# Plain queries and values in parts, and a new order of the first loads, in a fused attention and feed-forward kernel

## The chip, the cores and the metric

The kernel runs on one core of a Trainium2 chip. The metric is the device time of one execution in microseconds (us), the median of several runs. A core has five engines that run side by side: TensorE (PE: matmuls; PEld is its weight load), VectorE (DVE), ScalarE (ACT), GpSimd (POOL) and SyncE (SP), which here only issues DMA loads and stores. Each engine works off its own list in the order in which the program gives it and waits at semaphores for the others.

## The reference: what is computed

Eight batches with eight heads of 576 tokens and 64 columns go through windowed attention, and the result, 4608 rows of 512, through a feed-forward layer.

```python
mask_plain = (rel >= 0) & (rel < window)                                  # window 32, heads 0 to 3
mask_dil = (rel >= 0) & (rel < window * dilation) & (rel % dilation == 0)  # dilation 4, heads 4 to 7
...
scores = np.where(masks[None, :, :, :], scores, -1000000000.0)
attn = np.exp(scores - max);  attn = attn / sum(attn);  attn_out = attn @ v
...
h = x @ w_in                 # 512 -> 2048
g = np.maximum(0.01 * h, h)
return (g @ w_out)           # 2048 -> 512
```

Inputs and outputs are float32; the kernel computes in float16 operands with float32 sums.

## The kernel before

**Tiling.** Two batches share one activation buffer `xt` of 1152 token columns, which is cut into three chunks of 384. For each chunk the feed-forward layer runs 16 "ups" (`up`, L778: one block j of 128 hidden columns, four matmuls over the 512 inputs, weights `w_in`, result in a bank `hps`, leaky ReLU by ScalarE into `gt`, L803) and 12 "downs" (`down`, L827: three row tiles, each in four parts of four hidden blocks, weights `w_out`, L841). Chunk 0 holds the first 384 tokens of batch 0, chunk 1 those of batch 1, chunk 2 the last 192 tokens of both.

**Attention.** Heads come in pairs; a batch has two dilated pairs (hp 2, 3), then two plain pairs (hp 0, 1). Per pair, q and k are loaded into `stg`, cast to float16 in `nat` (L249), turned by TensorE into the bank `tp` (L557) and copied from there into `slots` (L507, L509). A unit of a pair is a score matmul into `sps` (L685; for the first two batches the mask is added by another matmul, L666), an exponential by ScalarE into `ee` (L691), for later units a mask multiply (L705), the value matmuls into `ops` (L729, L739, L749), and 1/sum as exp(-ln) by ScalarE into `rc` (L761, L763); the product goes into `xt` (L767). For batches 0 and 1 the units of the first 384 tokens ("part 0") come first, and the last 192 tokens ("part 1") later, with q and k reloaded in small pieces by `load_rest` (L389).

**Loads.** Nearly all loads go through one queue, issued by SyncE in a fixed order. The string `FIRST` (L20) gives the order of the early ones: b and v are q, k and values of batch 0 (dilated first, then plain), c and y the same of batch 1, i one of eight pieces of `w_in` (512 KB), o one of eight pieces of `w_out`, 0 and 1 the last tokens of a batch. `con` is a table of constants; its last part holds the mask multipliers. w_in pieces 1 to 4 hold hidden columns 0 to 1023 (ups 0 to 7), pieces 5 to 8 the rest; a piece gives 128 of the 512 inputs, so an up needs four pieces. Two pieces of w_out serve one part of the downs.

**Who sets the order.** The whole program is a list of tasks with engines, rough costs, dependencies and priorities. A planner (`_Plan.run`, L84) plays it through once while the kernel is built and so fixes each engine's order; nothing is reordered later. `RANKS` (L21) gives the priorities of the attention tasks of batch 0 part 0, part 1, batch 1 part 0, part 1 (start, step per pair). Where the planner expects a gap on TensorE before the first downs, it puts in filler matmuls on `warm` (L934), which compute nothing that is used.

Of the kernel before, what the change touches and what calls it, by code (L numbers as in the profile page):

```python
# [16 lines left out]
WHEN = (-5.0, 15.0, 50.0, 77.0, 112.0, 138.0, 172.0, 200.0)  # L17
CON = -1484.5
AFTER = -1495.0
FIRST = "bvbviiii0iicooiicoyoooooy1"  # L20
RANKS = ((10.0, 1.0), (10.0, 3.0), (20.0, 2.0), (40.0, 0.5))  # L21


def _constants():
# [113 lines left out]
def kernel(  # L138
# [94 lines left out]
                return n * (ta + (tb - ta) * (size - a) / (b - a)) / 16e3  # L233
        return n * size / 25.6 / 16e3

    def load(queue, dst, src, n, size, deps, prio):
        eng = ENG[queue]
        return plan.dma(queue, 0.7 if size == 128 else 0.48, took(n, size), deps,
                        lambda e: eng.dma_start(dst, src), prio,  # L239
                        LATE if prio > -1500 + len(FIRST) else 0.8 if prio >= AFTER else 0.0)  # L240

# [64 lines left out]
    def load_group(b, g, prio, prio_v):  # L306
# [28 lines left out]
        if dil and early:  # L335
            lv = [load("SP", at(vs, 0, 128, 0, [256, 4], [1, 256]),
                       dram(v, base, [4 * D, 128], [HS, 4], [1, 256]), 512, 1024, v_old, prio_v)]
            v_late[b] = vs, v_old, v_users
        elif dil:
            lv = [load("SP", at(vs, 0, 128, i * 256, [512, 4], [1, 256]),  # L340
                       dram(v, base + i * 64 * D, [4 * D, 128], [HS, 4], [1, 256]),
                       512, 1024, v_old, prio_v) for i in range(2)]
        elif early:
            lv = []
            for j in range(2):
                n = 12 - (first and j == 0)
                lj = [load("SP", at(vs, 0, 128, (12 * j + 12 - n) * D, [D, n], [1, D]),
                           dram(v, base + (1152 * j + 96 * (12 - n) - 32) * D, [D, 128], [96 * D, n],
                                [1, D]), 128 * n, 256, v_old, prio_v + 0.3 * j)]
                if n < 12:  # L350
                    lj += [load("SP", at(vs, PAD, 128, 0, [1, D]), dram(v, 0, [D, 96], [1, D]),
                                96, 256, v_old, prio_v), t_vz]
                lv.append(lj)
        else:
            lv = [load("SP", at(vs, 0, 128, 0, [D, 24], [1, D]),
                       dram(v, base - 32 * D, [D, 128], [96 * D, 24], [1, D]),
                       3072, 256, v_old, prio_v)]

        for j in range(2):
            nn, n_old = ring("NAT", NNAT, n_users := [])  # L360
            na, c_qk = nat[nn], []
            for o in range(2):
                st, s_users = stage[o]
                if early:
                    dst = at(na, 0, 128, o * 512, [D, 2], [128, 4], [1, D])
                    src = at(st, 0, 128, j * 512, [256, 2], [D, 4], [1, D])
                    n = 512
                else:
                    dst, src, n = na[:, o * S:o * S + S], st[:, j * S:j * S + S], S
                c_qk.append(cast(dst, src, n, (loads[o][j:j + 1] if first else loads[o]) + n_old, prio,  # L370
                                 (("ACT",) if o else ("DVE",)) if first and dil and j == 0 else
                                 CENG if early else ("POOL",)))
                s_users.append(c_qk[-1])
            dn, d_old = ring("VD" if dil else "VP", NV, d_users := [])
            vt = (vd if dil else vp)[dn]
            n_v = 384 if not dil else 256 if early else 512
            h_a, h_s = (2 * j * n_v, n_v) if early else (j * n_v, 2 * n_v)
            n, w = n_v // D, 128 * (8 if dil else 6)
            c_v = [cast(at(vt, 0, 128, 0, [w, 2], [128, n], [1, D]),
                        at(vs, 0, 128, h_a, [h_s, 2], [D, n], [1, D]), 2 * n_v,  # L380
                        (lv[j] if early and not dil else lv) + d_old, prio_v)]
            v_users += c_v
            seen_ones[b, 2 * g + j] = [t_ones["d" if dil else "p", dn]]
            kept[b, 2 * g + j] = vt, d_users
            visits[b, 2 * g + j, 0] = (na, c_qk, n_users, vt,
                                       c_v + ([t_one] if (b, 0) in TILED else
                                              [t_ones["d" if dil else "p", dn]]), d_users)

    def load_rest(b, prio):  # L389
# [5 lines left out]
        for o, src in ((0, q), (1, k)):  # L395
# [3 lines left out]
        c = cast(at(rest, 0, 128, 0, [128, 8], [D, 2], [1, D]),  # L399
                 at(st, 0, 128, 0, [D, 8], [0, 2], [1, D]), 1024, lo + r_old, prio)  # L400
        s_users.append(c)
        vs, v_old, v_users = v_late[b]
        spread = bass.AP(tensor=vs.tensor, offset=vs.offset + 1024,
                         ap=[[4 * vs.ap[0][0], 16], [256, 4], [1, 256]])
        lv = load("SP", spread,
                  dram(v, (b * H + 4) * HS + 512 * D, [4 * D, 16], [HS, 4], [1, 256]),
                  64, 1024, v_old + [t_vr], prio)
        for vi in (2, 3, 0, 1):
            vt, d_users = kept[b, vi]
            c_v = []  # L410
            if vi >= 2:
                c_v = [cast(at(vt, 0, 64, 0, [1024, 2], [128, 4], [1, D]),
                            at(vs, 0, 64, 1024 + (vi - 2) * 512, [256, 2], [D, 4], [1, D]), 512,
                            [lv] + d_users, prio + 30)]
                v_users += c_v
            visits[b, vi, 1] = rest, [c], r_users, vt, c_v + seen_ones[b, vi], d_users
# [3 lines left out]
    def load_w(n, prio):  # L420
# [10 lines left out]
        else:  # L431
            x = 1024 * (n - 8)
            src = dram(moe_w_out, 128 * x, [2 * DM, 128], [1, 1024])
            dst = w_out
        t = load("SP", st, src, 128, 4096, old, prio)
        for i in range(2):
            c = cast(dst[:, x + 512 * i:x + 512 * i + 512], st[:, 512 * i:512 * i + 512], 512, [t],
                     prio, ("POOL",) if 4 <= n < 8 else CENG)
# [71 lines left out]
        cost = {"DVE": 0.1 + n * 0.00065, "ACT": 0.08 + n * 0.00095}  # L510
        return add(tuple((e, cost[e]) for e in eng), None, 0.2, deps, fn, prio)

    slot_of, turned_rest, pair_moves = {}, {}, {}
    held = {t.name: [] for t in banks["S0"] + banks["O0"]}

    def arranged(dil, u0, u1):
# [6 lines left out]
    def turn(b, hp, part, prio):  # L523
# [50 lines left out]
        def k_to(bank, i, p0, p1, lo, hi, deps, eng=("DVE",)):  # L574
            n = hi - lo
            if dil:
                o, od, id_ = lo, [[144, 4], [1, n]], [[128, 4], [1, n]]
            else:
                o, od, id_ = PAD + 4 * lo, [[4, n], [1, 4]], [[1, n], [128, 4]]
            return [move(at(kb, p0, p1, o, *od), at(bank, p0, p1, i, *id_), 4 * n,  # L580
                         deps + old + zk, prio, eng)]

        if part == 1:
            if hp == 2:
# [26 lines left out]
            q_users += new  # L611
            ev += new
        else:
            _, q_old = ring("TP", 1, q_users := [])
            tq = add("PE", 0.23, 0.25, c_qk[:1] + [t_id] + q_old, turn_in(tpb, na, 0), prio, 0.2)
            n_users.append(tq)
            for lo, hi in ((0, 128),) if dil else ((0, 120), (120, 128)):
                q_users += q_to((lo, lo), lo, hi, [tq])
            if b == 0:
                _, k_old = ring("TPK", 1, k_users := [])  # L620
                kb_in, c_in, k_eng = tpk, 0, ("DVE", "ACT")
            else:
                k_old, k_users, kb_in, c_in, k_eng = q_old, [], tpb[:, 512:1024], 512, ("DVE",)
            tk = add("PE", 0.23, 0.25, [c_qk[1], t_id] + k_old, turn_in(kb_in, na, 512), prio, 0.2)
            n_users.append(tk)
            k_users += k_to(tpk if b == 0 else tpb, c_in, 0, 128, 0, 128,
# [3 lines left out]
            else:  # L630
                for t in q_users:
                    t.deps.append(tk)
                q_users += k_users
            ev += q_users + k_users
        slot_of[b, hp] = tn, users, ev
        return ev, users, qb, kb

# [347 lines left out]
```

The softmax here doesn't subtract the row's maximum and nothing guards it: scores larger than these inputs give would overflow.

## Time and profile before

| what | value |
|---|---|
| time, median of 3 runs | 317.56 us (317.21 to 317.59) |
| span of the profiled execution | 314.2 us |
| TensorE busy | 303.7 us (97%) |
| ScalarE / VectorE / GpSimd busy | 219.7 / 174.2 / 120.4 us |
| DMA queue of SyncE | 50.46 MB in 157,696 packets, 67.3% of 16 engines' span |
| chain that ended last | PE 83%, DMA 7%, ACT 4%, SyncE's queue 3% |

The page cuts the span into 40 slices of 7.85 us and gives the busy share of each engine as a digit (9 is 90% or more). A group or timeline line reads: start and length in us (timeline), engine, source line, operation, output tile <- input tiles, shape, count, and in brackets the idle time of the engine before it and who ended it. The answers by stage give the stretch, its length, and then the busy time of PE, PEld, DVE, ACT and POOL with the number of instructions in brackets, the granted clock of TensorE, the share of DMA engines busy and the data rate. The chain of waits gives start, length and the work that held the end back at that time.

### The profile page before, as it was taken

The numbers are of one execution on the slowest core, as the hardware profiler recorded it, in microseconds if no ns is written. First come the engines' busy times: TensorE is split into PE (matmuls) and PEld (weight loads), VectorE is DVE, ScalarE is ACT, GpSimd is POOL, SyncE is SP. The second block draws the span as 40 slices with busy tenths as digits, with TensorE's granted clock in tenths as the row PEclk, the third lists the DMA queues.
The fourth block names the chain that finished last, engine by engine and source line by source line (L and its number), as shares of the span: only waits on it lengthen the run. The fifth ranks groups of instructions, "written<-read, shape, count | busy, mean of one in ns | idle before, by whom it ended". The sixth has DMA issues, their size and how long they took to land.

```text
span 314.2 us, 6332 instructions
## 1 busy us (share of the span) xinstructions
PE 303.7 (97%) x2257; PEld 179.6 (57%) x2257; DVE 174.2 (55%) x396; ACT 219.7 (70%) x501; POOL 120.4 (38%) x174
## 2 busy tenths in 40 slices
PE   7968999999999999999999999999999999999995
PEld 3625555667777656655555555555555555555544
DVE  5856894557896687857858667654433420000011
ACT  3925674889998999987888888787887743334310
POOL 4466655464584463935819447450000000000000
PEclk9999999999999999999999999999999999999999
DMA  7999999999999399999989978711111111211113
GB/s 247 326 331 407 401 318 190 259 193 207 239 217 189 119 222 180 229 174 206 192 185 197 179 208 147 169 35 33 35 33 35 33 35 46 53 37 35 33 33 100
DMA packets 158175, 51.14 MB, mean 163 GB/s; under 512 B 139200, under 2 KB 151616, under 8 KB 158144
## 3 DMA queue, kind: packets, MB, share of 16 engines
q1 hardware_dynamic: 157696, 50.46, 67.3%
q8 instruction: 17, 0.28, 0.4%
q10 hardware_dynamic: 448, 0.29, 0.3%
q14 instruction: 14, 0.11, 0.1%
HBM read 41.30 MB, written 9.44 MB: 161 GB/s over the span
## 4 chain that ended last, share of the span: by engine, by line
PE 83%; DMA 7%; ACT 4%; SPq 3%; DVE 1%; issue 1%; POOL 0%; DVEq 0%
PE fps L841 38%; PE hps L792 36%; PE sps L685 3%; PE ops L749 3%; DMA wst<-in_moe_w_in_dram 3%; DMA con<-consts 3%; SPq L239 3%; ACT gt L803 1%; DMA stg<-in_k_dram 1%; ACT rc L761 1%; ACT rc L763 1%; PE ops L739 1%; PE sps L669 1%; DVE ee L705 1%; ACT ee L691 1%
## 5 line engine op out<-in xcount | busy, mean ns | idle before, releaser
L792 PE MATMUL hps<-xt,w_in 128*128 128x384 f16 (+1 forms) x824 | 149.9, 313 | 2.7 <-DVE w_in L249 1.3
L841 PE MATMUL fps<-w_out,gt 128*128 128x512 f16 (+1 forms) x592 | 145.7, 373 | 0.0
L803 ACT ACTIVATE gt<-hps 128x384 f16<-128x384 f32 (+1 forms) x206 | 94.0, 463 | 50.1 <-PE hps L792 46.1
L792 PEld LDWEIGHTS <-w_in 128*128 128x128 f16 x832 | 75.9, 98 | 46.0 <-DVE w_in L249 2.2
L841 PEld LDWEIGHTS <-gt 128*128 128x128 f16 x592 | 55.8, 98 | 45.1
L767 DVE TENSOR_TENSOR xt<-ops,rc 64x192 f16<-64x192 f32 (+2 forms) x138 | 52.4, 399 | 37.5 <-ACT rc L763 36.4
L544 POOL COPY slots<-turned 64x576 f16<-64x576 f16 x48 | 34.8, 724 | 59.6 <-DVE turned L539 47.0
L851 DVE COPY osb<-fps 128x512 f32<-128x512 f32 (+1 forms) x37 | 24.8, 671 | 55.7 <-PE fps L841 55.3
L705 DVE TENSOR_TENSOR ee<-ee,con 128x384 f16<-128x384 f16 x78 | 37.7, 487 | 30.9 <-ACT ee L691 29.7
L761 ACT ACTIVATE rc<-ops 64x384 f32<-64x384 f32 (+1 forms) x94 | 43.3, 464 | 13.7 <-PE ops L739 4.5
L691 ACT ACTIVATE ee<-sps 128x384 f16<-128x384 f32 x92 | 44.7, 486 | 9.8 <-PE sps L685 7.6
L763 ACT ACTIVATE rc<-rc 64x384 f32<-64x384 f32 (+1 forms) x96 | 46.7, 492 | 1.4
L249 POOL CAST nat<-stg 128x576 f16<-128x576 f32 (+1 forms) x52 | 34.9, 695 | 5.6 <-ACT ee L691 1.7
L685 PE MATMUL sps<-slots 128*128 128x192 f16 x152 | 25.0, 246 | 0.3 <-DVE slots L509 0.2
L685 PEld LDWEIGHTS <-slots 128*128 128x128 f16 x160 | 15.8, 102 | 11.7 <-issue 0.6
L249 POOL CAST vd<-vst 128x1024 f16<-128x1024 f32 (+2 forms) x20 | 17.5, 899 | 5.3 <-DMA vst<-in_v_dram 5.2
L550 DVE STREAM_TRANSPOSE slots<-nat 128x576 f16<-128x576 f16 x24 | 18.0, 762 | 1.3 <-POOL nat L249 1.1
L539 DVE STREAM_TRANSPOSE turned<-nat 128x576 f16<-128x576 f16 x24 | 18.1, 763 | 0.1
L509 DVE COPY slots<-tp 64x128 f16<-64x128 f16 (+5 forms) x47 | 14.4, 320 | 5.3 <-PE tp L557 4.6
L749 PEld LDWEIGHTS <-vp 128*128 128x128 f16 x160 | 11.1, 98 | 5.6
L249 POOL CAST vp<-vst 128x768 f16<-128x768 f32 x16 | 13.1, 832 | 2.9 <-DMA vst<-in_v_dram 2.2
L749 PE MATMUL ops<-ee,vp 128*128 128x96 f16 x160 | 13.3, 206 | 0.0
(64 smaller groups left out, 131.2 us busy)
## 6 DMA issues: line engine op xcount, KB each, us to landing
vst<-in_v_dram SPq DMA_DIRECT2D x14, 512.0 KB, 5.0
stg<-in_q_dram SPq DMA_DIRECT2D x48, 144.0 KB, 3.8
stg<-in_k_dram SPq DMA_DIRECT2D x48, 144.0 KB, 2.9
vst<-in_v_dram SPq DMA_DIRECT2D x6, 768.0 KB, 5.9
out_dram<-osb SPq DMA_DIRECT2D x16, 192.0 KB, 2.3
gt<-in_moe_w_in_dram SPq DMA_DIRECT2D x5, 512.0 KB, 7.0
out_dram<-osb SPq DMA_DIRECT2D x24, 96.0 KB, 2.1
out_dram<-osb SPq DMA_DIRECT2D x14, 128.0 KB, 2.6
```

The costliest lines, as they stand in the source:

```text
L249: ENG[e].tensor_copy(out=dst, in_=src)
L544: lambda e, p0=p0, hh=hh: nc.gpsimd.tensor_copy(out=at(qb, p0, p0 + 64, hh * S + o, *od), in_=at(xb, p0, p0 + 64, i, *id_)), prio)
L685: nc.tensor.matmul(st[:, 192 * i:192 * i + 192], ka, qa, start=not by_pe, stop=i == 1 or not by_pe)
L691: lambda e: nc.scalar.activation(out=et, in_=st[:, 0:384], func=AF.Exp, scale=SCALE), prio + 0.1)
L705: ENG[e].tensor_tensor(out=io, in0=io, in1=mk, op=ALU.mult)
L749: nc.tensor.matmul(ot[:, c:c + 96], va, et[:, c:c + 96], start=True, stop=True)
L761: lambda e: nc.scalar.activation(out=r_out, in_=r_in, func=AF.Ln), prio + 0.2)
L763: lambda e: nc.scalar.activation(out=r_out, in_=r_out, func=AF.Exp, scale=-1.0),
L767: nc.vector.tensor_tensor(out=dst, in0=at(ot, p0, p1, c, *i_), in1=at(rt, p0, p1, c, *i_), op=ALU.mult)
L792: nc.tensor.matmul(ht[:, 0:n], at(w_in, 0, 128, i * DFF + j // 2 * 256 + j % 2, [2, 128]), at(xt[m % 2], 0, 128, i * 1152 + x0 + x, [1, n] ...
L803: lambda e: nc.scalar.activation(out=gt[c % NG][:, j * n_c + x:j * n_c + x + n], in_=ht[:, 0:n], func=AF.Prelu, alpha=0.01),
L841: nc.tensor.matmul(ft[:, 0:n_o], g[:, j * n_c + tt * 128:j * n_c + tt * 128 + 128], w_out[:, j * DM + c0:j * DM + c0 + n_o], start=(j == 0 ...
```

## The change: q and values of the plain heads in parts, another order of loads

It aims at the first 35 us, in which loads and the first attention units have to be done before the feed-forward layer can run without waiting:

- Values of the plain heads (batches 0 and 1) are loaded per head, four of the six 128-row tiles ahead, tiles 4 and 5 later together with the last tokens; the casts are cut in the same way.
- In batch 0 the q of both plain pairs is turned into one bank together, only the part for the first 384 tokens is copied at once, the rest later for both pairs in shared copies. The k copy of the second pair is left to VectorE.
- The loading order puts the first w_in piece ahead of plain values and the next behind them, and the first w_out piece, the third w_in piece and the last tokens ahead of the fourth w_in piece. The fifth w_in piece stays ahead of batch 1's q and k; the sixth goes behind them.
- `RANKS` has other priorities for the attention tasks, and the planner counts the first four w_in pieces 1.35 times as long.

In the order that the planner makes of it, the loads after batch 0's q and k are:

```
before: v plain (all) | w_in 1 2 3 4 | last q k v | w_in 5 6 | q k of batch 1 | w_out 1 2 | w_in 7 | con | w_in 8 | q k plain | w_out 3 | v
after:  w_in 1 | v plain (4 of 6 tiles) | w_in 2 | w_out 1 | w_in 3 | last q k v, plain v rest | w_in 4 5 | q k of batch 1 | w_out 2 | w_in 6 7 | con | w_in 8 | q k plain | w_out 3 | v
```

```diff
-FIRST = "bvbviiii0iicooiicoyoooooy1"
-RANKS = ((10.0, 1.0), (10.0, 3.0), (20.0, 2.0), (40.0, 0.5))
+FIRST = "bvbivioi0oiiciiicoyoooooy1"
+RANKS = ((-100, 0.5), (5, 1), (20.0, 0.5), (20, 3))
...
         elif early:
             lv = []
-            for j in range(2):
-                n = 12 - (first and j == 0)
...
+            for h in range(4):
+                t0 = int(first and h == 0)
+                lv.append([load("SP", at(vs, 0, 128, (6 * h + t0) * D, [D, 4 - t0], [1, D]),
+                                dram(v, base + h * HS + (96 * t0 - 32) * D, [D, 128],
+                                     [96 * D, 4 - t0], [1, D]),
+                                128 * (4 - t0), 256, v_old, prio_v + 0.1 * h)])
...
+            lv = [lv[0] + lv[1], lv[2] + lv[3]]
+            v_late[b, 0] = vs, v_old, v_users
...
+        ps, p_old, p_users = v_late[b, 0]
+        lp = [load("SP", at(ps, 0, 128, t * D, [6 * D, 4], [1, D]),
+                   dram(v, b * H * HS + (96 * t - 32) * D, [D, 128], [HS, 4], [1, D]),
+                   512, 256, p_old, prio) for t in (4, 5)]
...
-        t = load("SP", st, src, 128, 4096, old, prio)
+        t = load("SP", st, src, 128, 4096, old, prio, 1.35 if n < 4 else 1.0)
...
+            if b == 0 and not dil:
+                if hp == 0:
+                    _, q_old = ring("TP", 1, q_users := [])
+                    both = []
+                    for x in range(2):
+                        n_x, c_x, u_x = visits[b, x, 0][:3]
+                        both.append(add("PE", 0.23, 0.25, c_x[:1] + [t_id] + q_old,
+                                        turn_in(tpb[:, 512 * x:512 * x + 512], n_x, 0), prio, 0.2))
+                        u_x.append(both[-1])
+                    two_q.append((both, q_users))
+                tq, q_users = two_q[0]
+                x = 512 * hp
+                made = q_to((x, x), 0, 96, tq)
+                q_users += made
...
+            if (b, hp) == (0, 1):
+                k_eng = ("DVE",)
...
+            if b == 0 and hp == 1:
+                later = []
+                for hh in range(2):
+                    p0 = 64 * hh
+                    for i, n, c in ((96, 24, 384), (120, 8, 480)):
+                        later.append(move(
+                            at(qbd[tn - 1], p0, p0 + 64, hh * S + c, [2 * S, 2], [24, 4], [1, n]),
+                            at(tpb, p0, p0 + 64, i, [512, 2], [128, 4], [1, n]), 8 * n,
+                            tq + zq + t_zero[tn - 1][0], prio + 30))
```

## The prediction

> **What bounds the kernel now.** I read the slices of the page first, then the chain of waits over the first 45 us, then the timeline between 31 and 37 us, then busy times by stage.
>
> ```profile
> PE   7968999999999999999999999999999999999995
> DMA  7999999999999399999989978711111111211113
> ```
>
> TensorE is full from slice 6 on and DMA is full until slice 23. Slices are 7.85 us, so whatever a change of the loading order can win lies in the first 40 to 45 us. The same stretch by stage (PE busy is the second figure, the DMA rate the last):
>
> ```profile
> 15.00:20.00 5.00, 3.32 (x25) 1.47 (x23) 2.51 (x8) 2.06 (x7) 2.41 (x4) 1.00 0.98 323
> 20.00:25.00 5.00, 3.73 (x26) 2.13 (x27) 2.18 (x10) 2.17 (x6) 4.50 (x7) 1.00 1.05 360
> 25.00:30.00 5.00, 4.29 (x39) 2.58 (x37) 3.95 (x13) 2.69 (x6) 3.04 (x6) 1.00 1.05 415
> 35.00:40.00 5.00, 4.63 (x42) 3.09 (x41) 4.02 (x12) 4.90 (x13) 2.86 (x6) 1.00 1.05 409
> 45.00:60.00 15.00, 15.00 (x126) 8.34 (x125) 9.78 (x29) 8.52 (x24) 6.84 (x10) 1.00 0.94 207
> ```
>
> Busy flatters TensorE: the filler matmuls on `warm` alone take 1.9 us between 18 and 30 us. In the chain four 512-column matmuls take 0.86 us, so 0.42 ns a column. Counting columns, fillers left out, at that rate gives 285.9 us of needed work in a span of 314.2 us. The lost time has reached 17.5 us at 34 us, 18.5 us at 45 us, 18.6 us at 60 us. It then creeps up by some 5.5 us over 250 us. Both kernels have the same 285.9 us, so the change wins only what it takes off the lost time.
>
> ```profile
> 12.74 8.72 DMA wst<-in_moe_w_in_dram
> 21.52 0.87 POOL w_in L249
> 23.15 8.68 DMA con<-consts
> 31.92 2.12 DVE ee L705 x4
> ```
>
> The fourth piece of w_in lands at 21.5; the last part of `con` (the masks) at 31.83; four masks follow on VectorE. The timeline goes on:
>
> ```profile
> 33.16 0.68 POOL L249 CAST w_in<-xt 128x512 f16<-128x512 f32 x1 [0.28 <-DMA xt<-in_moe_w_in_dram]
> ...
> 33.81 0.87 ACT L761 ACTIVATE rc<-ops 64x384 f32<-64x384 f32 x2 [3.30 <-PE ops L739]
> 33.82 1.46 PE L792 MATMUL hps<-xt,w_in 128*128 128x384 f16 x8
> ...
> 35.66 0.40 PE L557 MATMUL tp<-con,nat 128*128 128x128 f16 x4 [0.37 <-DVE nat L249]
> ```
>
> The eighth w_in piece lands at 33.1, its first half is cast at 33.84, and ups 8 to 15 of chunk 0 start at 33.82. At 35.3 TensorE stands before a transpose of batch 1's plain q, which waits for a cast that VectorE reaches only after the masks and three slot copies. After that TensorE is full.
>
> **What the Trainium skill says.** DMA: Bandwidth & Descriptors, Issuing engines are not separate DMA queues: all DMAs share the same 16 engines. The trace agrees: transfers land in the order of issue, so a load put ahead delays all behind it by its own service. Same page, Why small descriptors are slow: small packets carry a fixed cost. Here 12 x 128 rows of 256 B (384 KB) took 1.24 us (landings 12.36 and 13.61), where 512 KB in 1 KB rows took 1.26 (25.12 to 26.38). TensorE: Matmul & The Clock Gate, The mechanism: matmuls keep program order, so one early wait stalls all behind it. The trace agrees as far as I looked: the matmuls of the timeline stand in the program's order, and up 10 follows the late transpose at 35.66. Trace Analysis, Identifying the Most-Contended Engine: matmul busy is no measure of headroom. The trace agrees (303.7 us busy against 285.9 counted).
>
> **The change, part by part.**
>
> *Plain values in parts.* Ahead go 4 of 6 tiles of each head: about 2,000 rows of 256 B instead of 3,040, a third of 2.5 us, so 0.83 us leaves the early stream and returns with the last tokens. It adds issues of about 0.5 us each on SyncE, hidden, since that engine runs ahead (first w_in piece issued 9.99, landed 15.9). The two casts of 0.83 us on GpSimd become about 0.61 each (row of 128x512) early and two of about 0.33 later, among idle time.
>
> *Plain q copies.* Eight copies for two head pairs before (1.20 us per pair), eight after; only 384 tokens of each are copied early (four of about 0.33), the rest later. The key copy of the second pair goes to VectorE alone (about 0.69 there, 0.60 off ScalarE). All this precedes the first up, which waits for weights, so it costs nothing.
>
> *Start of chunk 0.* The first w_in piece (1.25 us by the later rate, 2.3 by its own landing gap 13.61 to 15.92) goes ahead of plain values. The last key load ends about 11.0, so the second value half lands at 11.0 + 1.25..2.3 + 2,000 x 0.81 ns = 13.9 to 14.9 instead of 13.6. Before, the last xt piece came 4.2 us after it (17.88), now 18.1 to 19.1. Ups 0 to 3 need the third piece anyway (19.74 before, about the same now, since 512 KB of w_out in and 0.83 us of values out almost cancel). Cost: nothing.
>
> *Fourth w_in piece.* Ahead of it now lie the first w_out piece (1.25), the last tokens of q, k and v (0.8) and the rest of plain values (0.83), less the 0.83 saved: 21.5 + 2.0 = 23.5. Cast 0.87: 24.4. From there to up 8 TensorE has 7.0 us of columns, plus about 1 us for evictions: 32.4. Up 8 still needs the eighth piece at 33.1, so about 1.4 us of delay is free. Before, this stretch held 7.5 us of columns in 11.4 us, with fillers.
>
> *The late stream.* Counted in order, the bytes ahead of `con` and ahead of the eighth piece are **the same** in both kernels: only their order differs (fifth piece and batch 1's q and k hardly move, the sixth comes 4.8 us later, the second w_out piece 1.7 us earlier). So masks start at 31.9 and up 8 at 33.8 as before. The columns ahead of up 8 are equal too (16.2 us).
>
> *From up 8 on.* The first two down parts now run at 29.5 to 31.8 (second w_out piece at 28.6), not at 31.4 to 33.6. So the values of the last tokens no longer queue behind them: they start at 32.5 (masks), not 33.2, and ScalarE's logarithms at 32.9, not 33.8. Batch 1's plain transposes move behind up 13, so the stall of 0.38 us before them, and its 0.6 us of lost time, goes. Instead ScalarE takes both reciprocals and an exponential before the eviction of up 8 (its new order): 32.9 + 5 x 0.45 = 35.15, eviction to 35.6, so up 10 starts at 35.65, not 35.89. ScalarE has 19 operations from there to the eviction of up 15 in both orders and starts 0.9 us earlier. TensorE gets 0.24 us at up 10, and at most the 0.95 us lost between 34 and 45 us. I take about two thirds of that, 0.6 to 0.7.
>
> **The rivals.**
>
> *The stream itself gets faster.* From 13.61 to 23.85 five pieces and 320 KB took 10.2 us; at 1.25 a piece and 0.8 they need 7.1. About 3.1 us were lost in slow packets, most beside the first four w_in pieces. If they suffer from following each other, breaking them up may return half: 1.6 us off the masks and up 8, giving 315.9. Against: the slow stretch also holds 1 KB packets of other loads, which speaks for a time, not for a tensor.
>
> *A new wait takes the place of the old one.* Up 10 stands behind two evictions that ScalarE now does later in its order. With ScalarE at 4.90 of 5 us between 35 and 40 us this can eat all: no change, 317.4.
>
> *Slower.* The slack ahead of up 8 shrinks from over 3 us to 1.4. If the fourth piece lands at 25.5 instead of 23.5 (its own gap was already 1.75), ups 0 to 7 finish late and each further microsecond is on TensorE. Later the key copy of batch 1's second pair stands on VectorE behind casts of q and k landing at 34.4 and 35.7, which bring it to about 37.9, just when TensorE asks for it. 0.5 to 1.5 us: 318.5.
>
> **The numbers.** The forecast (same stream, stall gone, part of it lost to ScalarE) has 0.42: 317.56 - 0.65 = 316.9, of which 0.30 is beyond 0.2% (0.64 us) and 0.12 within. The faster stream 0.20, no change 0.14, slower 0.24 (0.01 within). Together 0.50 faster, 0.27 the same, 0.23 slower. The range goes from the faster stream with a little more, 315.6, to the slower case, 318.4.
>
> **What would show it.** Up 8 within 0.4 us of 33.8 and masks at 31.9 show the equal stream; a fourth piece near 23.5 its cost; the value matmuls of the last tokens near 32.5, and no wait for a nat cast behind up 9, the gain; an idle stretch of TensorE behind up 9, ended by ScalarE, the new wait. The forecast is wrong if the eighth piece moves by over 0.5 us, if TensorE idles between ups 0 to 7 and up 8 for a weight other than the eighth piece, or if lost time after 45 us differs by over 0.5 us.

## The result: 1.4 us slower, and the profile after

The kernel after takes **318.94 us** (median of 4 executions, 318.78 to 318.96), the kernel before 317.57 beside it (317.21 to 317.61): ratio **1.0044, 95% interval 1.0027 to 1.0062**. A second comparison, on another occasion, gave 318.05 against 316.5 and again 1.0044 (1.0019 to 1.0070). The forecast was 316.9, with a range of 315.6 to 318.4: the kernel became slower, not faster, and its time lies outside the range.

Single executions of one kernel differ by more than the change does, in part by the clock that TensorE was granted: of 59 of the kernel before (315.69 to 319.99 us) 39 had a mean clock of 0.997 or more, with a median of 316.56 us, and 20 had less, with a median of 318.08, so that two traces of either kernel are compared below and ratios come from many executions. The trace that the prediction read belongs to a quick one (315.94).

The slices of the page of after:

```profile
PE   8778999999999999999999999999999999999995
DMA  7999999999999899889979979811111111111113
```

As before, TensorE is at 90% or more from slice 5 on (the prediction has slice 6), and the DMA engines are busy up to slice 26. The same stages as before, busy times of the kernel after (columns: whole stretch, PE, PE weight loads, DVE, ACT, POOL, clock, DMA share, GB/s):

```profile
15.00:20.00 5.00, 4.20 (x40) 2.25 (x41) 2.52 (x11) 3.17 (x10) 1.33 (x3) 1.00 0.98 327
20.00:25.00 5.00, 3.22 (x22) 1.65 (x22) 3.36 (x14) 0.00 (x0) 4.36 (x7) 1.00 1.02 319
25.00:30.00 5.00, 3.62 (x23) 1.87 (x22) 3.32 (x10) 2.29 (x6) 4.49 (x9) 1.00 1.06 388
35.00:40.00 5.00, 4.35 (x48) 2.72 (x46) 4.45 (x12) 4.37 (x11) 3.21 (x5) 1.00 1.07 399
45.00:60.00 15.00, 14.65 (x136) 8.09 (x134) 12.79 (x39) 8.10 (x23) 6.71 (x11) 1.00 0.97 205
```

The stream moves less in each of the stages shown from 20 to 40 us (319, 388, 399 GB/s; before 360, 415, 409). Of the second pair of traces that is true of one stage only (a_again 346, 377, 406; b_again 320, 411, 410). VectorE has 12.8 us of work between 45 and 60 us where it had 9.8. ScalarE has none at all from 20 to 25 us: it waits for the first evictions.

Four places of the kernel after decide. **First**, the early issues on SyncE (timeline; SPq is its queue):

```profile
7.06 0.34 SPq L239 DMA_DIRECT2D gt<-in_moe_w_in_dram  x1
7.44 3.97 SPq L239 DMA_DIRECT2D vst<-in_v_dram  x5
11.49 1.88 SPq L239 DMA_DIRECT2D gt<-in_moe_w_in_dram  x1
```

The second w_in piece stands behind five loads of plain values. Its issue begins at 11.49, and lasts 1.88 us where the first one's lasts 0.34. In this execution the queue also waits for landings; its waits up to 12 us:

```profile
SPq L239 <- DMA stg<-in_q_dram: 1.5, 2, 1.1
SPq L239 <- DMA vst<-in_v_dram: 0.9, 1, 0.9
SPq L239 <- DMA stg<-in_k_dram: 0.8, 2, 0.5
```

The program gives eight semaphores to its loads in turn, so that an issue waits until the load eight places before it has landed: the first w_in piece is issued at 7.06, just behind the landing of an early load of q at 7.04. Over the same stretch the first trace of before has one such wait, of 0.6 us, its second two of 0.5; the second trace of after has 2.0 us in all.

**Second**, the chain of waits between 22 and 28 us:

```profile
22.83 1.25 POOL rest L249
24.07 0.05 issue
24.12 0.64 PE tp L568 x8
24.76 0.02 issue
24.78 0.57 DVE slots L520 x2
...
26.67 0.60 DVE w_in L249
27.27 0.05 issue
27.32 0.35 PE hps L837
```

The fourth w_in piece landed at 24.31, but VectorE's half of its cast comes only at 26.67, behind the slot copies of the last tokens; these wait for TensorE's transposes, these for GpSimd's cast of the last q and k. TensorE goes on with ups 0 to 3 at 27.32 and is dense from there to up 8.

**Third**, behind up 9 (timeline):

```profile
37.68 0.32 PE L711 MATMUL sps<-con 128*128 128x384 f16 x1 [0.65 <-ACT ee L736]
```

The wait for a nat cast at this place is gone, and TensorE stands for 0.65 us for ScalarE's exponential in its stead.

**Fourth**, the chain at 53 to 57 us, where that of the kernel before had TensorE's own work alone. First before, then after:

```profile
55.04 1.30 PE hps L792 x8
56.34 0.17 PE sps L669 x4
56.51 1.30 PE hps L792 x8
```

```profile
53.21 0.46 PE tp L568 x8
53.67 0.02 issue
53.70 0.57 DVE slots L520 x2
...
56.13 0.36 DVE xt L812
56.49 0.03 issue
56.52 0.23 DVE slots L520
56.75 0.03 issue
56.78 0.37 DVE ee L750
57.15 0.04 issue
57.20 0.36 PE ops L784 x8
```

The last tokens of batch 1's plain heads stand earlier now, so TensorE comes to their value matmuls before VectorE has copied, scaled and masked, and stands for 0.4 us.

Lost time is counted as in the prediction, at 0.4167 ns a column; needed work is 285.87 us in all these kernels. "10 MB" is when the transfers that have ended hold 10 MB (2^20 bytes each); "4th" is the first up matmul that needs the fourth w_in piece; the last two columns are lost time at 44 us, and what is lost from there to 100 us. Each row is one trace; the ratio to before is from all executions of that comparison. The column behind it takes the medians of the executions at full clock alone, this kernel's over before's, with the number of this kernel's. Full clock is taken as a mean of 0.997 or more, since the traces that show no lower clock until the last instructions have means of 0.998 to 1.000.

| kernel | traced us | ratio to before | at full clock | 10 MB | 4th | up 8 | lost at 44 | 44 to 100 |
|---|---|---|---|---|---|---|---|---|
| before | 315.94 | 1 | 1 | 32.03 | 22.44 | 33.82 | 18.29 | 1.57 |
| before, again (b_again) | 317.76 | 1 | 1 | 32.69 | 22.82 | 35.46 | 20.00 | 1.60 |
| after | 318.93 | 1.0044 | not on record | 34.35 | 27.32 | 35.43 | 20.48 | 2.16 |
| after, again (a_again) | 318.05 | 1.0044 | 1.0046 (10) | 33.28 | 26.16 | 34.72 | 19.47 | 2.24 |
| castfirst | 318.10 | 1.0039 | 1.0047 (15) | 33.59 | 25.17 | 34.82 | 19.68 | 2.03 |
| rank4 | 317.30 | 1.0032 | 1.0035 (18) | 32.69 | 25.61 | 34.01 | 18.83 | 2.08 |
| w1act | 316.79 | 1.0001 | 1.0006 (16) | 31.53 | 25.38 | 33.49 | 18.61 | 1.97 |
| both | 315.90 | 0.9959 | 0.9989 (22) | 31.70 | 23.83 | 32.33 | 17.23 | 2.67 |
| bothrank | 314.66 | 0.9949 | 0.9956 (9) | 31.08 | 22.94 | 31.64 | 16.37 | 1.92 |
| b_act | 315.91 | 0.9977 | 0.9987 (19) | 31.41 | 21.78 | 33.70 | 18.29 | 1.57 |
| b_split | 318.49 | 1.0073 | 1.0079 (2) | 33.42 | 24.17 | 36.24 | 20.64 | 1.33 |
| firstnew | 322.11 | 1.0118 | 1.0049 (1) | 31.93 | 27.71 | 38.11 | 22.40 | 3.36 |
| vwhole | 317.67 | 1.0038 | 1.0045 (5) | 32.34 | 24.49 | 34.15 | 18.77 | 3.15 |
| vw_rank | 320.54 | 1.0056 | 1.0064 (11) | 34.16 | 27.05 | 36.18 | 20.75 | 3.76 |
| best2 | 318.03 | 1.0024 | 1.0041 (22) | 30.68 | 23.47 | 33.63 | 18.29 | 3.63 |

Two traces of each kernel give 19.1 and 20.0 us lost at 44 us on average, and 1.6 and 2.2 between 44 and 100 us. So **about 0.8 us of the loss lies ahead of 44 us and about 0.6 behind**. The first figure comes from traces that differ by more than that among themselves; the second is steady (1.57 and 1.60 against 2.16 and 2.24). From 100 to 300 us the kernels lose nearly the same (4.3 us in both traces of before, 4.4 in both of after). At full clock the distance between the kernels is 1.46 us (317.72 against 316.25), so it isn't the clock's.

**The stream falls behind at a second place**, from 28 to 32 us. The DMA engines are about as busy there as in the kernel before, and carry a fifth less (b_again, then a_again; the DMA share and GB/s stand last):

```profile
28.00:32.00 4.00, 2.45 (x23) 1.48 (x22) 3.21 (x7) 1.47 (x3) 1.92 (x4) 1.00 1.03 413
28.00:32.00 4.00, 3.86 (x35) 2.47 (x33) 1.64 (x5) 3.29 (x8) 2.44 (x5) 1.00 1.00 332
```

The first traces have 406 and 327 GB/s. In this second pair the stretch is all of the lateness: by 28 us a_again has moved 8.22 MB and b_again 8.14, by 32 us 9.50 and 9.73. castfirst (333), rank4 (343) and w1act (355) have the slow stretch too, both (400) and vwhole (408) don't. What slows the transfers there is not shown.

### The profile page after: what moved, and what is told of

It is laid out like the page before. It is cut to its first block, busy times and chain, and to the rows that moved or that the text cites. A ratio compares the mean times of both kernels' runs of the same rounds, so it can differ in the third digit from the quotient of the medians.

```text
span 317.1 us, 6349 instructions
## 1 busy us (share of the span) xinstructions
PE 305.2 (96%) x2259; PEld 180.1 (57%) x2259; DVE 174.5 (55%) x397; ACT 219.6 (69%) x501; POOL 119.2 (38%) x177
## 4 chain that ended last, share of the span: by engine, by line
PE 85%; DMA 6%; ACT 3%; DVE 2%; issue 1%; POOL 1%; SPq 0%; POOLq 0%
PE hps L837 37%; PE fps L886 37%; PE sps L730 4%; DMA vst<-in_v_dram 3%; PE ops L794 3%; DMA stg<-in_k_dram 2%; DVE slots L520 1%; ACT ee L736 1%; PE ops L784 1%; DMA stg<-in_q_dram 1%; ACT gt L848 1%; ACT rc L808 1%; PE tp L568 1%; ACT rc L806 1%; PE sps L714 1%
## 5 line engine op out<-in xcount | busy, mean ns | idle before, releaser
L750 DVE TENSOR_TENSOR ee<-ee,con 128x384 f16<-128x384 f16 x80 | 37.5, 473 | 31.8 <-ACT ee L736 30.8
L249 POOL CAST nat<-stg 128x576 f16<-128x576 f32 (+1 forms) x53 | 35.7, 697 | 5.4 <-DMA stg<-in_q_dram 1.9
L520 DVE COPY slots<-tp 64x128 f16<-64x128 f16 (+7 forms) x47 | 14.2, 319 | 5.3 <-PE tp L568 4.8
L249 POOL CAST vp<-vst 128x768 f16<-128x768 f32 (+2 forms) x20 | 13.7, 708 | 1.9 <-DMA vst<-in_v_dram 1.2
```

The lines of the kernel that those rows point to most:

```text
L249: ENG[e].tensor_copy(out=dst, in_=src)
L750: ENG[e].tensor_tensor(out=io, in0=io, in1=mk, op=ALU.mult)
```

## The experiments

Three theories stood at the start, under these names. HOLE: the stream is late because the second w_in piece is held on SyncE's queue while the engines drain. CAST: the fourth piece's cast on VectorE, late behind the slot copies, makes TensorE's dense work end late. CHANCE: both kernels take the same time ahead of 45 us, and the traces differ as executions do. LATE came after the first four runs: the fourth place above.

**b_again: the kernel before once more**, without an edit.

> The kernel before, unchanged, for a second trace. Theory HOLE (the load stream of the changed kernel runs dry for about 1.5 us behind the plain values; before it doesn't): no 0.5 us stretch before 40 us with the 16 DMA engines under 50% busy, con landing between 31.5 and 33.0, eighth w_in piece between 32.8 and 34.3. Rival CHANCE (the first trace of before was an untypically quick one, span 314.2 against 317.56 us timed): a span near 315.8, and the stream late by 1 to 2 us at the eighth piece, so that part of the 2.0 us between the two traces is not the change's.

317.76 us; 20.00 us are lost at 44 us, 1.7 more than in the first trace, and the masks start at 33.72. The wait for the masks, which I had first read as the change's doing, can be as late without it.

**w1act: the second w_in piece from ScalarE's queue.** In `load_w` of after:

```diff
         t = load("SP", st, src, 128, 4096, old, prio, 1.35 if n < 4 else 1.0)
+        if n == 1:
+            t.fn = lambda e: nc.scalar.dma_start(st, src)
```

> The changed kernel with one thing altered: the second w_in piece is issued from ScalarE's DMA queue instead of SyncE's, in the same place of the planner's time; all other lists stay. Theory HOLE: SyncE's issue of this piece waits (11.5 to 13.4 us) until the slowest DMA engine has worked off the small rows of the values, and meanwhile the others have nothing; from the other queue it is there in time, so the hole at 13 to 14.5 us goes, con and the eighth piece land about 1.3 us earlier, and the time falls by 1.0 to 1.5 us to about 317.6. Rival CAST (TensorE is late because the fourth piece's cast stands behind eight slot copies on VectorE): the stream gets earlier but the time falls by less than 0.5 us.

Ratio **1.0001** (0.9978 to 1.0024): the whole loss is gone, 1.4 us (at full clock 1.0006). The timeline of this kernel shows the issue of the piece at 8.89, and not at 11.49 (10.62 in the second trace of after), and over in 0.44 us:

```profile
5.92 0.47 SPq L239 DMA_DIRECT2D gt<-in_moe_w_in_dram  x1
6.44 4.24 SPq L239 DMA_DIRECT2D vst<-in_v_dram  x5
8.89 0.44 ACTq L448 DMA_DIRECT2D gt<-in_moe_w_in_dram  x1
```

10 MB are there at 31.53, 1.8 and 2.8 us sooner than in the two traces of after. The edit does two things at once: the piece has a queue of its own, and it now goes ahead of three of the five loads of values and lands at 14.32, not at 17.25 or 17.05. No run puts it there on SyncE's queue, so which of the two gives the gain is not shown.

**castfirst: the late cast put ahead.** In after, behind the planner:

```diff
     order = plan.run()
+    first_copy = min(t.start for t in pair_moves[0, 2])
+    for t in w_used[3]:
+        if t.eng == "DVE":
+            t.start = first_copy - 1e-6
+    order.sort(key=lambda t: (t.start, t.n))
```

> The changed kernel with one thing altered: on VectorE the cast of half of the fourth w_in piece stands ahead of the eight slot copies of the last tokens instead of behind seven of them; all other lists stay. Theory CAST: the cast starts at 24.4 instead of 26.7, ups 0 to 7 start about 1.5 us earlier and the time falls by over 0.8 us. Theory HOLE: up 8 is held by the eighth piece at 35.1 anyway, ups 0 to 7 only end earlier and fillers or idling take the gain: within 0.4 us of 318.9.

1.0039 (1.0023 to 1.0056), and 1.0047 at full clock: no gain that can be told. The fourth pass starts at 25.17, not at 26.2 to 27.3, but up 8 still waits for the eighth piece (34.82).

**both: the two edits together.**

> The changed kernel with both alterations: second w_in piece from ScalarE's queue, fourth piece's cast ahead of the slot copies. HOLE and CAST together (two bounds that end at the same time): the time falls by 1.5 to 2 us, to 317.2 or below, clearly more than either alone. HOLE alone: the same as with the piece on ScalarE's queue alone, within 0.3 us.

**0.9959** (0.9939 to 0.9979), where w1act has 1.0001. Part of this distance is the clock: all 22 executions of both had full clock, of w1act's 22 only 16. At full clock both is 0.5 us under w1act (316.21 against 316.75; resampling the executions gives 0.2 to 1.0) and 0.35 us under before. So the early cast, which gave nothing alone, gives half a microsecond on top of the second queue. The chain of waits says why. In w1act the stream has been repaired, and the chain through the cast decides:

```profile
20.33 1.25 POOL rest L249
21.58 0.05 issue
21.63 0.63 PE tp L570 x8
...
24.18 1.16 DVE w_in L249
25.34 0.05 issue
25.38 0.35 PE hps L839
```

In both, that chain is out of the way, and a transfer decides, that of the masks:

```profile
22.64 8.18 DMA con<-consts
30.82 0.03 issue
...
30.92 1.17 DVE ee L752 x2
```

In after the two ended together: the eighth piece was cast from 35.19, and TensorE came to up 8 at 35.4 with its dense work. **Two paths of nearly equal length hide each other's cost.**

**rank4: the last tokens of batch 1 back at their old place.** In after:

```diff
-RANKS = ((-100, 0.5), (5, 1), (20.0, 0.5), (20, 3))
+RANKS = ((-100, 0.5), (5, 1), (20.0, 0.5), (40.0, 0.5))
```

> Edit: in the kernel after, only the last pair of RANKS goes back from (20, 3) to (40.0, 0.5), so that the work on the last tokens of batch 1's plain heads stands later in every engine's program; the program of TensorE is the same up to about 50 us. LATE (the work stands too early, TensorE comes to its value matmuls at 53 to 58 us before VectorE has turned, masked and scaled): the 1.0 us of lost time between 44 and 59 us goes and stays gone, about 0.1 to 0.2 there as before the change; the ratio to before falls from 1.0044 to about 1.001 (317.9 us). STREAM ONLY (the loss that counts is the one before 45 us; what is saved at 59 us is given back later, because the same waits come when the work does stand there): lost time between 44 and 100 us unchanged at about 3.7 us, ratio 1.004.

1.0032 (1.0016 to 1.0047), an interval that holds after's 1.0044. Its trace has no wait for VectorE at 53 to 58 us, and loses 2.08 us between 44 and 100 us all the same (after 2.16 and 2.24): the wait was real, and taking it away was nearly worthless here. My expectation of 0.1 to 0.2 us there fell.

**bothrank: the three edits together.**

> Edit: the kernel after with three edits: the second w_in piece issued on ScalarE's queue, VectorE's half cast of the fourth piece ahead of the eight slot copies of the last tokens, and the last pair of RANKS back at (40.0, 0.5). If the losses of the stream, of the late cast and of the late part add up: the first two gave 0.9959 of before, the third gives 1.0 us more, ratio 0.993 (315.0 us), lost time at 59 us about 17.5. If the late part is only the stream's and the cast's loss seen again, 0.996, as the kernel with the first two.

0.9949 (0.9918 to 0.9980), 315.08 us: the quickest kernel of this study, under before by half a per cent, and short of the sum that was expected (0.993). From 0.9959 the interval can't tell it. Two things speak for a part of the third edit. The trace of both has a wait of 0.80 us for VectorE at 54 us and loses 2.67 us between 44 and 100 us; that of bothrank has no such wait and loses 1.92. And at full clock bothrank is 1.4 us under before, both 0.35. The two were compared with before on different occasions, so this part is likely, but not shown.

**b_act: the second queue in the kernel before.**

```diff
         t = load("SP", st, src, 128, 4096, old, prio)
+        if n == 0:
+            t.fn = lambda e: nc.scalar.dma_start(st, src)
```

> Edit: the kernel before, with one edit: its first w_in piece (the one that follows the second half of plain values and its 256 B rows) is issued on ScalarE's queue and not on SyncE's. HOLE (the time that the second queue gives in the kernel after comes from an issue on SyncE that was held until the rows ahead of it had drained; in the kernel before over a thousand descriptors were still ahead when the issue of the first piece ended, so nothing drained): no change, ratio 0.999 to 1.001, stream at 10 MB moved still at 32.0 to 32.7 us. SECOND QUEUE ANYWAY (two queues carry the pieces faster than one, whatever holds the issue): stream at 10 MB 0.5 to 1 us sooner, ratio about 0.997, and then the change to the order costs the full difference to the best kernel after.

0.9977 (0.9961 to 0.9993), and at full clock 0.9987 (resampled: 0.9975 to 1.0001). The theory that only an issue held until the engines ran dry costs time fell, by the ratio over all executions and by the 10 MB at 31.41: here nothing ran dry, and the second queue still gave 0.7 us, 0.4 at full clock. Here too the piece lands earlier, at 13.46 and not at 15.92. So of w1act's 1.4 us a third to a half is no cure of the change, but a gain that the kernel before could have had as well.

**b_split: the early loads of plain values of before in halves.** Same bytes, rows and plan:

```diff
+                def halves(j, n):
+                    def fn(e):
+                        for x, w in ((0, n - 6), (n - 6, 6)):
+                            nc.sync.dma_start(
+                                at(vs, 0, 128, (12 * j + 12 - n + x) * D, [D, w], [1, D]),
...
+                lj[0].fn = halves(j, n)
```

> Edit: the kernel before with each of the two early loads of plain values (1,408 and 1,536 rows of 256 B) issued as two loads of half the tiles; same bytes, same rows, same plan, all else the same. The program gives eight semaphores to its loads in turn, so that each issue waits until the load eight places before it has landed. LOOK-AHEAD (more and smaller loads shorten what SyncE can have under way, as the parts of plain values do in the kernel after): waits of SyncE's queue on landings up to 12 us rise from 0.6 to 1.0 us (before) to 1.5 us or more, the stream has moved 10 MB later by 0.3 to 1 us (32.7 to 33.3), ratio 1.001 to 1.003. ROWS (only the bytes and the rows count, not how many loads they are in): stream at 10 MB at 32.0 to 32.7 and ratio 0.999 to 1.001.

**1.0073** (1.0053 to 1.0093): two more issues for the same bytes cost 2.3 us, more than either theory said. Four of the six executions had a lower clock, but the two at full clock took 318.60 and 318.92, 2.5 us over before's, so the cost isn't the clock's. 10 MB come at 33.42. The waits on landings up to 12 us did not rise (0.6 us). What shows is the timeline of SyncE's queue; first the kernel before, then b_split:

```profile
5.91 4.04 SPq L239 DMA_DIRECT2D vst<-in_v_dram  x3
9.99 2.23 SPq L239 DMA_DIRECT2D gt<-in_moe_w_in_dram  x2
```

```profile
6.06 1.87 SPq L353 DMA_DIRECT2D vst<-in_v_dram  x2
7.97 1.88 SPq L239 DMA_DIRECT2D vst<-in_v_dram  x1
9.89 1.55 SPq L353 DMA_DIRECT2D vst<-in_v_dram  x2
11.49 1.10 SPq L239 DMA_DIRECT2D gt<-in_moe_w_in_dram  x2
```

The first w_in piece is issued at 11.49, not at 9.99, since five issues of values take 5.4 us where three took 4.0. But its own issue then takes 0.63 us and not 1.75, and the second piece follows at 12.16, not at 11.79. Nor does this later issue explain the delay: b_again issued its second piece at 12.12 and had it at 17.81, b_split has it at 19.68. So the cost of more loads is shown, and that it needs no longer waits on landings up to 12 us; the way by which it comes is open.

**firstnew: the new order of loads alone**, in the kernel before:

```diff
-FIRST = "bvbviiii0iicooiicoyoooooy1"
+FIRST = "bvbivioi0oiiciiicoyoooooy1"
```

> Edit: the kernel before with the new order of early loads alone (the new FIRST; plain values whole, q copies and RANKS old). This is the order without the other parts. HOLE with CAST: the second w_in piece again follows 256 B rows of plain values and its issue is held; the fourth piece lands about 1 us later still because the values are whole; up 8 waits for an eighth piece at 34.5 to 35.5 us; without the loss at 53 to 58 us: 0.5 to 1.2 us over before, ratio 1.002 to 1.004. PARTS (the 256 B rows in parts and the copies are what costs, not the order): ratio 0.999 to 1.001.

1.0118 (1.0073 to 1.0163), three times what was expected or more. The stream is not late (31.93), but with whole values and the old plan the fourth pass starts at 27.71 and up 8 at 38.11. Much of this is TensorE's clock. In the trace TensorE stands for 3.52 us behind its first up matmul, and afterwards the granted clock is half, from 20.7 to 31.0 us (timeline, then busy times, clock third from the end):

```profile
22.18 1.76 PE L792 MATMUL hps<-xt,w_in 128*128 128x384 f16 x5 [3.52 <-DVE xt L767]
21.00:31.00 10.00, 7.82 (x30) 3.99 (x30) 8.87 (x23) 2.13 (x5) 8.85 (x14) 0.50 1.04 400
```

Five of the six executions have a mean clock of 0.984 to 0.995 (318.73 to 322.11 us). The one at full clock took 318.03, 1.0049 of before's, about as much as the whole change costs. So that the other parts of the change win something back from the order shows only with the clock counted in.

The other traces fit. The one other kernel whose trace has TensorE idle for over 2 us between 10 and 40 us is b_split (2.44 us from 18.0); its clock is half from 22.7 to 26.1. The other 13 traces have at most 1.84 us and full clock until the last instructions. Over all executions, 9 of 12 of these two kernels had less than full clock; 75 of 261 of the kernels whose longest idle stretch is 1.3 to 1.8 us (before, after, castfirst, rank4, w1act, b_act); and 1 of 70 of those with at most 1.1 us (both, bothrank, vwhole, vw_rank, best2). So shorter gaps of TensorE and a kept clock go together, and the ratios over all executions hold both. That one brings the other is not tested by a run.

**a_again: after once more.**

> The kernel after once more, unchanged, for a second trace. In its first trace SyncE waited 1.1 us for the landing of an early q piece before it could issue the first w_in piece (7.06 instead of about 6.0 in the other kernels with the same early order), and 0.9 us for a values piece, and the stream then ran dry at 13 us. If that belongs to the kernel, the ratio to before is again 1.003 to 1.006 and the stream has moved 10 MB at 33.5 to 34.5 us. If it was chance in one execution, 10 MB at 32.6 to 33.0, and the ratio about 1.002 to 1.003, from the late cast and from the wait at 57 us that remain.

1.0044 again, so the loss belongs to the kernel. In this trace nothing ran dry and the first piece was issued at 6.22; 10 MB are still late, at 33.28. So the dry microsecond of the first trace isn't part of every execution of after; vw_rank's trace has one as well (203 GB/s from 12 to 16 us).

**vwhole: after with plain values whole.** The loop of before over two loads takes the place of the four, and the two late loads and their casts go:

```diff
-            for h in range(4):
...
-            v_late[b, 0] = vs, v_old, v_users
+            for j in range(2):
+                n = 12 - (first and j == 0)
...
-        lp = [load("SP", at(ps, 0, 128, t * D, [6 * D, 4], [1, D]),
...
```

> Edit: the kernel after with plain values loaded whole again in two loads (and the 96 rows), all six tiles of a head early, nothing of them with the last tokens; the new order, the new RANKS and the q copies stay. Two issues fewer ahead of the second w_in piece's successors, 0.83 us of rows more ahead of it. LOOK-AHEAD: fewer loads, fewer waits of SyncE on landings, and the eighth piece is not later than in the kernel after: ratio 1.002 to 1.005. BYTES (the rows ahead of the second to fourth piece decide, as the order alone with whole values gave 1.0118): ratio 1.007 or more, most of it lost between 18 and 34 us.

1.0038 (1.0023 to 1.0052), so here BYTES fell. At full clock it is 1.0045, and after 1.0046: taking the parts back changes nothing in the whole. Its planner puts the cast of the fourth piece ahead of the slot copies by itself, and 10 MB are there at 32.34. It loses as much as after, but elsewhere: 3.15 us between 44 and 100 us.

**vw_rank: vwhole with the old place of batch 1's last tokens** (the edit of rank4).

> Edit: the kernel after with plain values whole (as in vwhole) and, in addition, the last pair of RANKS back at (40.0, 0.5). In vwhole the early part is as good as before the change: the stream has moved 10 MB at 32.34 us, and VectorE casts the fourth w_in piece ahead of the slot copies; its trace loses 3.1 us between 44 and 100 us where the kernels before lose 1.6. LATE (that loss comes from the place of batch 1's last tokens): lost time between 44 and 100 us falls to 2.0 us or less, the ratio from 1.0038 to about 1.000. GIVEN BACK (what is saved there is lost at the next waits): still 2.8 us or more by 140 us after 44 us, and the ratio stays at 1.003 to 1.004.

1.0056 (1.0036 to 1.0076), and 3.76 us lost from 44 to 100 us: GIVEN BACK. The trace is of the slowest of its 12 executions (320.54; median 318.39). In it the wait for VectorE at 56 us is gone, and TensorE stands a little further on, for ScalarE (timeline of vw_rank):

```profile
58.73 0.33 PE L703 MATMUL sps<-slots 128*128 128x96 f16 x4 [0.58 <-ACT ee L725]
```

**best2: vw_rank and the second queue** (the edits of rank4, vwhole and w1act).

> Edit: vw_rank with the second w_in piece issued on ScalarE's queue. If whole values, the second queue and the old place of batch 1's last tokens add up, the ratio is 0.995 or below, as in the best kernel so far (bothrank, 0.9949), which keeps the values in parts: then the parts of the values bring nothing of their own. If the parts are worth their 0.83 us of rows moved out of the early stream, 0.997 to 0.999.

1.0024 (1.0004 to 1.0045), at full clock 1.0041: neither of the two. With values in parts the same set of edits and the early cast gave 0.9949, 0.7% less. This speaks for the parts once a second queue is there, but does not single them out: the two kernels have different plans, and of the 3.6 us that best2's trace has lost more by 100 us, 1.9 lie ahead of 44 us and 1.7 behind.

## Why the prediction was wrong

**The step that failed first: "It adds issues of about 0.5 us each on SyncE, hidden, since that engine runs ahead".** The size held: the five early issues of values took 0.37 to 0.57 us each. "Hidden" did not. The lead of SyncE was read from one piece (issued 9.99, landed 15.9), but the second w_in piece, which the new order puts behind these five, is issued at 11.49 and 10.62 in the two traces and holds SyncE for 1.88 and 1.82 us. Moving that one issue to the other queue took the whole loss away (w1act, 1.0001), and in the kernel before two more issues for the same bytes cost 2.3 us (b_split). So issues on SyncE are on the path; by which way, whether the place, the queue or the packets that travel together, is open. The trace of before held a warning: its three issues of plain values took 4.04 us, 2.99 of them the load of 96 rows behind that of 1,408.

**"... about the same now, since 512 KB of w_out in and 0.83 us of values out almost cancel".** The third piece landed at 22.08 and 21.20, not near 19.74. The sum took 1.25 us, the later rate, for the w_out piece ahead of it; from the landing of the second w_in piece to its own it took 3.3 and 2.5 us. The prediction knew the slow packets of this stretch, but only as time to be won.

**"The bytes ahead of `con` and ahead of the eighth piece are the same … So masks start at 31.9 and up 8 at 33.8 as before."** The bytes are the same; time per byte isn't. 10 MB came 0.6 to 2.3 us later, pair by pair, much of it in the slow stretch from 28 to 32 us. The eighth piece, by the prediction's own sign of failure, moved by over 0.5 us (cast from 35.19 and 34.56; before 33.16 in the trace that was read). The second trace of before has it at 34.95, so of this distance the traces show nothing for certain: I took a quick execution for the kernel.

**"Fourth w_in piece … 23.5. Cast 0.87: 24.4."** The landing was near: 24.31 and 23.88. The cast was not: VectorE's half ended at 27.27 and 26.10. The forecast took GpSimd's duration and left out VectorE's own order, with slot copies ahead that wait for TensorE's transposes and GpSimd's cast. This ate the 1.4 us of slack. Of the rival *Slower* that is the mechanism (ups 0 to 7 finish late), but by the cast rather than by the landing. That its size, 318.5, comes near is luck: castfirst took the late cast away and gained nothing.

**"From up 8 on": the forecast gain.** The wait for a nat cast behind up 9 (0.38 us in the trace read, 0.53 in the second) did go. What came was the rival *A new wait takes the place of the old one*: 0.65 and 0.54 us for ScalarE's exponential. So "I take about two thirds of that" is the term that was mis-sized: it measured nothing.

**"Lost time after 45 us" the same.** 0.6 us more, a loss that no experiment took away as a whole. One wait in it is named (0.4 us at 57 us, TensorE for VectorE); in rank4 and vw_rank moving it away only moved it, in bothrank it seems to have helped. The traces fall into three groups. With the old order 1.3 to 1.6 us are lost there; with the new order and values in parts 1.9 to 2.7; with the new order and whole values 3.2 to 3.8. The last group holds firstnew, which differs from before by the order of loads alone, so there the loss came with the order and not with the new `RANKS`, and the parts seem to lessen it. Apart from before and after, each kernel has one trace, and firstnew's has half clock until 31 us. Why the loss comes is **open**.

**What held.** The first 18 us cost almost nothing (lost time at 18 us: before 10.85 and 11.01, after 11.41 and 11.17). Whether the intended gain exists is not settled. With the second queue and the early cast the new order is at 0.9959 of before, and at 0.9949 with the old place of the last tokens, while the old order with a second queue is at 0.9977. The intervals overlap, and at full clock the three are 0.9989, 0.9956 and 0.9987: only bothrank is ahead, by 1.0 us of b_act on the same occasion (315.08 against 316.06; resampled 0.2 to 1.5). That speaks for a gain once the costs are out of the way.

Of the Trainium skill, DMA: Bandwidth & Descriptors, Issuing engines are not separate DMA queues, I used that all transfers share the same engines. The section also says that issuing from several engines "will only save the time on the sequencer it takes to initiate the DMA, which is usually small relative to the DMA itself". Here it was not small: one piece of 512 KB moved to the second queue gave 0.7 us in the kernel before (0.4 at full clock) and 1.4 us in after. Left open is which share of this is the shorter issue, which the earlier place of the piece, and which the mixing of 4 KB packets among the 256 B rows while they drain.

## What to carry to other kernels

A split of a load isn't free because its bytes stay the same: read in the timeline of the issuing queue how long the issues behind many-row loads last and what stands behind them, and run the split alone. When two paths end at the same instruction, here the eighth weight piece and TensorE's own dense work, undo them together before calling either harmless. When a wait is moved off the path, look at what the engine meets next: two of the waits taken away here came back at another instruction. And before an edit is given its ratio, compare the granted clock of the executions on both sides.

## What the runs showed of the hardware that I had not expected

- An issue's length on SyncE depends on what stands ahead of it in its queue, and not on that alone. Behind a load of 1,408 rows of 256 B the next issue took 2.77 to 3.06 us in six traces (1.60 in best2); behind 1,536 rows 1.75 us in the kernel before, and 2.65 to 3.06 in the four kernels with the new order and whole values. In b_split, with those rows in halves, the long ones took 1.34, 1.88 and 1.08 us. Most issues of that time took 0.34 to 0.79 us.
- Which queue issues one piece moved the whole stream: all five traces with one w_in piece on ScalarE's queue have 10 MB at 30.7 to 31.7 us, all ten with SyncE's queue alone at 31.9 to 34.4.
- Two executions of the same kernel can differ by 1.8 us at full clock, nearly all of it ahead of 44 us (before: 18.29 and 20.00 us lost there), with the landing of `con` at 31.8 in one and about 33.6 in the other.
- TensorE's granted clock fell to half in the two traces that have it idle for over 2 us between 10 and 40 us (2.44 us: half clock for 3.4 us; 3.52 us: for 10.2), and in none of the 13 others (at most 1.84 us idle).
- DMA engines that are almost equally busy can carry 332 or 413 GB/s in the same 4 us (a_again and b_again, 28 to 32 us).
